# One core, eight batches of two-way attention and a gated convolution block: a new order of the same operations on every engine

## The chip, the cores and the metric

The kernel runs on one core of a Trainium2 chip. The metric is device time in microseconds (us) of one execution; the profile's times count from the start of its span. Five engines work side by side, each through its own list of instructions in order: TensorE (PE in the profile, its weight loads PEld), VectorE (DVE), ScalarE (ACT), GpSimd (POOL) and SyncE (SP), which here only issues transfers.

## The reference

The inputs are x (8 batches, 8 heads, 512 rows, 64 columns) and state (8, 8, 32, 64). Each head reads the state with its rows and the rows with its state, both by a softmax; the 544 rows of each batch then pass a hidden layer, a convolution over three neighbouring rows, a gate and an output layer.

```
scores = scale * x @ state.T ; a = softmax(scores) ; xread = a @ state
scores2 = scale * state @ x.T ; a2 = softmax(scores2) ; sread = a2 @ x
x = concatenate([xread, sread])          (8, 544, 512), heads side by side
h = maximum(x @ w_in, 0)                 (8, 544, 1024)
conv_out = sum over k of conv_w[k] * h shifted by k - 1 rows
out = (h * sigmoid(conv_out)) @ w_out    (8, 544, 512)
```

## The kernel before

All work is written first as a plan of 1,673 operations (class Plan), each a function with its engine, what it reads and what it writes. Two tables at the head of the file turn the plan into a program. ORDER lists the operations by number in the order in which they are issued; each engine, SP among them, keeps the part of the list that is its own. A number with a v gives an operation to VectorE that otherwise is ScalarE's, and -n stands for idle multiplications on TensorE of n times 128 columns, with no use for the result (function fill, line 231). BANKS says which of the eight PSUM banks each PSUM tile takes, in the order of the tiles. Waits follow from these tables: an instruction waits for what it reads, and for the last reader of the buffer or bank that it overwrites.

The weights come first (w_load, line 255; five small operations on ACT and DVE for each of 17 pieces), with the attention of batches 0 to 3 beside them. For each batch b the second softmax (scores2) goes through these steps:

- scores (PE, line 323), keep_scores (ACT, line 208), top (DVE, line 352), exp2 (ACT, line 361).
- For batches 4 to 7 the exponentials are turned on a round trip through DRAM, two tiles per batch, 2b and 2b+1: turn (DVE transposes 32x32 blocks, line 378, tile tv), away (SP issues the transfer far<-tv, line 382), and lay (SP issues the transfer e2t<-far, line 386, which waits for that away to land).
- x_load (SP, line 315, tile xx, two halves of 512 KB per batch, two buffers), then read (PE, line 399, tile ps_r) multiplies xx with both tiles e2t of its batch. The batches come to read in the order 0, 2, 1, 3, 5, 7, 6, 4.
- divide, read_flip and read_flipped bring the result to the tile sr, and state_hidden (PE, line 660) makes the hidden rows of the state from it.

The first softmax (softmax, lines 475 to 499) goes over 1024 columns on DVE, with one exponential and one copy on ACT. state_product (PE, line 593) multiplies the state with w_in in its place, so that hidden (PE, line 675, six matmuls) needs only the softmax and that product.

The main body are 64 steps i = 8b + f, one per batch and block f of 128 hidden columns: hidden on PE, relu (ACT, line 214), middle (ACT, line 208, or DVE), before and behind (DVE, lines 718 and 723), sigmoid (ACT, line 727), gate (DVE, line 732), gate_high (ACT, line 219), gate_low (DVE, line 222), then four times project (PE, line 750, three matmuls), one for each chunk c of 128 rows. After the last block of a batch, end (ACT, line 770, or DVE, line 772) brings the sum of chunk c out of PSUM into a tile o, and store (SP, line 791) sends it to the output. There are two buffers o, so an end waits until the store of an earlier one has landed. The last batch stores halves; its last product (project_part, line 755) writes one half of a bank, and end of the other half reads the same bank.

All transfers but three (conv_w and two of the last stores) are issued by SP, strictly in its own order: a store whose tile is not ready holds up every away, lay and x_load behind it, and an away or lay holds up the stores behind it.

```
    def away(i):
        far[i] = dram.tile([P, S], F32, tag="far", name=f"far_{i}")
        nc.sync.dma_start(far[i], tv[i])

    def lay(i):
        e2t[i] = buf([P, 4, NCH * NS], F32, "e2t", f"e2t_{i}")
        nc.sync.dma_start(e2t[i], far[i].rearrange("(h s) (j m) -> (s j) h m", s=NS, j=4))
```

Of the kernel before, what the change touches and what calls it, by code (L numbers as in the profile page):

```python
# [1011 lines left out]
```

## Time and profile before

| | us |
|---|---|
| three runs: median (lowest to highest) | 365.69 (364.69 to 366.98) |
| the profiled execution, whole | 366.53 |
| its span, first to last instruction | 364.8 |
| busy in the span: PE, PEld, DVE, ACT, POOL | 346.9, 270.7, 318.0, 253.3, 39.4 |

Of the 366.53 us of the profiled execution 1.7 lie around the span. The windows view gives busy time by engine in stretches of the span, the granted clock of TensorE and the share of the transfer engines; the chain follows the work that ended last back to its releasers; the timeline lists instructions in order, with the idle time before them in brackets.

### The profile page before, as it was taken

The page shows a single profiled execution, that of the slowest core. Times are in us where ns is not written, and L with a number is a line of the kernel's source. Part 1 is how long each engine was busy: PE and PEld are TensorE (multiplying, and loading weights), DVE is VectorE, ACT ScalarE, POOL GpSimd, SP SyncE. Part 2 cuts the span into 40 slices and gives each one's busy share as a digit, 9 for nine tenths or more (in the row PEclk, how much of TensorE's full clock was granted, in tenths as well). Part 3 has the DMA queues.
Part 4 walks back from the last instruction along what each step waited for, and adds up shares of the span by engine and source line. Part 5 has one row for each costly group of instructions (what it writes and reads, how often), then busy time and mean ns, then how long its engine had stood idle before and what let it go on. Part 6 is the DMA issues. An engine that isn't in the chain of part 4 may idle for free.

```text
span 364.8 us, 6597 instructions
## 1 busy us (share of the span) xinstructions
PE 346.9 (95%) x2493; PEld 270.7 (74%) x2493; DVE 318.0 (87%) x547; ACT 253.3 (69%) x552; POOL 39.4 (11%) x90
## 2 busy tenths in 40 slices
PE   7899979999899989997699999999999999999995
PEld 4767648788588858874598887887788868888874
DVE  1999997999999987999299999999988987998861
ACT  2999979998767776866475659346885575457632
POOL 1000000140000000412000332001031021021100
PEclk9999999999999999999699999999999999999999
DMA  7999795343320065225210001012000030001105
GB/s 259 397 368 363 249 375 188 108 153 86 123 84 0 35 197 201 70 78 173 89 58 0 2 0 59 1 58 88 30 1 2 0 117 0 0 8 47 63 0 173
DMA packets 19343, 39.24 MB, mean 108 GB/s; under 512 B 1904, under 2 KB 8176, under 8 KB 19312
## 3 DMA queue, kind: packets, MB, share of 16 engines
q1 hardware_dynamic: 18880, 38.54, 30.5%
q8 instruction: 19, 0.31, 0.4%
q10 hardware_dynamic: 432, 0.29, 0.3%
q14 instruction: 12, 0.10, 0.1%
HBM read 27.81 MB, written 11.01 MB: 106 GB/s over the span
## 4 chain that ended last, share of the span: by engine, by line
PE 77%; DMA 9%; DVE 6%; ACT 6%; issue 1%; SPq 1%; DVEq 0%; ACTq 0%
PE acc L750 37%; PE ps_h L675 19%; PE ps_hs L660 4%; PE ps_h L682 4%; PE acc_t L750 3%; DMA out<-o 3%; DMA xx<-xn 2%; PE ps_u L593 2%; PE ps_r L399 2%; DMA far<-tv 2%; PE ps_s L323 2%; DMA raw<-w_in 2%; PE acc_c L750 1%; DVE t L723 1%; DVE t L718 1%; ACT hc L259 1%
## 5 line engine op out<-in xcount | busy, mean ns | idle before, releaser
L750 PE MATMUL acc<-wo,g 128*128 128x512 f32 x723 | 173.2, 390 | 0.0
L750 PEld LDWEIGHTS acc<-wo,g 128*128 128x128 f32 x723 | 135.0, 188 | 28.5 <-DVE g L222 0.4
L675 PE MATMUL ps_h<-a,u 128*128 128x512 f32 x336 | 84.5, 398 | 0.0
L675 PEld LDWEIGHTS ps_h<-a,u 128*128 128x128 f32 x336 | 64.1, 193 | 15.9 <-ACT hs L664 0.8
L727 ACT ACTIVATE t<-t 128x512 f32<-128x512 f32 x64 | 39.8, 629 | 23.5 <-DVE t L723 23.1
L219 ACT ACTIVATE g<-t 128x512 fp32r<-128x512 f32 (+1 forms) x62 | 37.8, 618 | 18.5 <-DVE t L732 12.7
L718 DVE SCALAR_TENSOR_TENSOR t<-h,cw,t 128x511 f32<-128x511 f32 x64 | 47.1, 744 | 1.3 <-ACT t L208 1.2
L723 DVE SCALAR_TENSOR_TENSOR t<-h,cw,t 128x512 f32<-128x512 f32 (+1 forms) x64 | 47.0, 745 | 0.7
L222 DVE TENSOR_TENSOR g<-t,g 128x512 fp32r<-128x512 f32 (+1 forms) x62 | 41.3, 669 | 5.8 <-ACT g L219 5.7
L732 DVE SCALAR_TENSOR_TENSOR t<-t,h 128x512 f32<-128x512 f32 (+1 forms) x64 | 41.8, 662 | 4.7 <-ACT t L727 4.6
L214 ACT ACTIVATE h<-ps_h 128x512 f32<-128x512 f32 x58 | 34.2, 595 | 13.0 <-PE ps_h L675 11.5
L208 ACT ACTIVATE t<-h,cw 128x512 f32<-128x512 f32 x52 | 37.3, 722 | 2.9 <-DVE h L216 1.9
L693 POOL COPY hs<-h 128x1 f32<-128x1 f32 x40 | 17.0, 440 | 173.1 <-ACT h L214 149.8
L770 ACT ACTIVATE o<-acc 128x512 f32<-128x512 f32 (+1 forms) x30 | 16.3, 558 | 17.0 <-DMA out<-o 9.6
L693 POOL COPY h<-hs 128x1 f32<-128x1 f32 x40 | 17.6, 461 | 58.7 <-DVE t L732 37.2
L222 DVE TENSOR_TENSOR u<-ps_u,u 128x512 fp32r<-128x512 f32 x28 | 18.8, 679 | 3.2 <-ACT u L219 3.2
L399 PEld LDWEIGHTS ps_r<-xx,e2t 128*32 128x32 f32 x512 | 8.3, 115 | 17.6 <-DMA e2t<-far 3.8
L399 PE MATMUL ps_r<-xx,e2t 128*32 128x64 f32 x512 | 9.9, 229 | 11.0 <-DMA e2t<-far 5.2
L219 ACT ACTIVATE u<-ps_u 128x512 fp32r<-128x512 f32 x28 | 16.0, 595 | 1.1 <-PE ps_u L593 0.8
L660 PEld LDWEIGHTS ps_hs<-sr,wi 128*128 128x128 f32 x128 | 14.9, 192 | 1.4 <-ACT at L208 0.8
L660 PE MATMUL ps_hs<-sr,wi 128*128 128x128 f32 x128 | 15.3, 276 | 0.0
L259 ACT ACTIVATE hc<-raw 128x512 f32<-128x512 f32 (+1 forms) x17 | 11.2, 664 | 5.5 <-DMA raw<-conv_w 2.8
(103 smaller groups left out, 402.7 us busy)
## 6 DMA issues: line engine op xcount, KB each, us to landing
xt<-xT SPq DMA_DIRECT2D x16, 512.0 KB, 6.9
xx<-xn SPq DMA_DIRECT2D x16, 512.0 KB, 5.8
out<-o SPq DMA_DIRECT2D x27, 256.0 KB, 2.1
raw<-w_in SPq DMA_DIRECT2D x8, 512.0 KB, 7.3
raw<-w_out SPq DMA_DIRECT2D x8, 512.0 KB, 7.5
far<-tv SPq DMA_DIRECT2D x8, 256.0 KB, 2.8
e2t<-far SPq DMA_DIRECT2D x8, 256.0 KB, 3.1
out<-o SPq DMA_DIRECT2D x6, 128.0 KB, 1.8
```

The costliest lines, as they stand in the source:

```text
L208: A.activation(dst, src, AF.Copy, scale=scale)
L214: A.activation(dst, src, AF.Relu, scale=0.5)
L219: A.activation(hi, src, AF.Copy)
L222: engine.tensor_tensor(lo, src, hi.bitcast(F32), op=ALU.subtract)
L660: PE.matmul(ps_hs[m, f][:, :NT], wi[:, k, f * P:(f + 1) * P], sr[m][:, k, :], start=(k == 0), stop=(k == NK - 1))
L675: PE.matmul(ps_h[i], u[j][:, g, fs], a[k][:, g, :], start=(n == 0), stop=(n == 3 * NG - 1))
L693: G.tensor_copy(dst, src)
L718: V.scalar_tensor_tensor(t[:, 1:], h[:, :S - 1], cw[:, f, 0:1], t[:, 1:], op0=ALU.mult, op1=ALU.add)
L723: V.scalar_tensor_tensor(t[:, :n], h[:, 1:n + 1], cw[:, f, 2:3], t[:, :n], op0=ALU.mult, op1=ALU.add)
L727: A.activation(tt[i], tt[i], AF.Tanh, scale=0.25)
L732: V.scalar_tensor_tensor(tt[i][:, :n], tt[i][:, :n], 1.0, hd[i][:, :n], op0=ALU.add, op1=ALU.mult)
L750: PE.matmul(acc, g[j][:, cs], wo[:, k, f, :], start=(f == 0 and n == 0), stop=(f == end and n == 2))
```

## The change

Both tables are replaced; nothing else in the file differs. The operations are the same but for idle multiplications: 12 entries instead of 6, all of them in the first 20 us of work, six more instructions of 128 columns. VectorE takes 24 operations from ScalarE in both (9 middle, 7 relu, 7 end and 1 keep_scores, where it was 12, 6, 5 and 1). The start of the new order and two lines of the tables:

```diff
 ORDER = """
-99 100 -1 121 -5 -7 102 101 103 122 1 -1 125 15 126 -1 127v 143 0 104 16 18 17 144 19 128 21 22 24 151 145 3 2 152 153
+0 -1 -5 122 121 99 100 -7 -1 -1 -1 -1 101 102 103 104 -1 1 125 127v 15 16 126 128 17 143 18 151 144 145 21 23 129 19 3
...
-1511 1522v 1462 1508 1477 1523 1492 1520v 1521 1507 1518 1519
+1508 1663 1477 1524 1525 1517 1662 1492 1507 1518 1520v 1521 1519
```

What the change moves is shown at three places. In the names, far_15 and e2t_15 are the round trip of tile 15 (batch 7, tile 1), xx_7_0 is the first half of x for batch 7, and o_1_2_0 is the output tile of batch 1, chunk 2; the last number of a name only counts tiles.

SP in the middle of the program, before, around the two round trips of batch 7:

```order
L382 DMA far_15_1616<-tv_15_1611 128x512
L386 DMA e2t_15_1634<-far_15_1616 128x4x128
L791 DMA out<-o_0_2_0_1231 128x512
L315 DMA xx_7_0_1674<-xn 128x1x1024
L382 DMA far_14_1695<-tv_14_1668 128x512
L791 DMA out<-o_1_2_0_1697 128x512
L386 DMA e2t_14_1741<-far_14_1695 128x4x128
L315 DMA xx_6_0_1794<-xn 128x1x1024
```

The same place in the change:

```order
L382 DMA far_14_1572<-tv_14_1561 128x512
L382 DMA far_15_1600<-tv_15_1587 128x512
L386 DMA e2t_15_1664<-far_15_1600 128x4x128
L386 DMA e2t_14_1681<-far_14_1572 128x4x128
L315 DMA xx_7_0_1689<-xn 128x1x1024
L791 DMA out<-o_1_1_0_1715 128x512
L791 DMA out<-o_1_2_0_1776 128x512
```

Both far transfers of batch 7 now come first, then both e2t, then xx, and the stores of batch 1 stand behind them; before, a store of batch 0 and one of batch 1 stood between.

SP at the two round trips of batch 4 (tiles 8 and 9), before:

```order
L382 DMA far_8_2039<-tv_8_2037 128x512
L386 DMA e2t_8_2044<-far_8_2039 128x4x128
L315 DMA xx_4_1_2085<-xn 128x1x1024
L315 DMA xx_4_0_2091<-xn 128x1x1024
L382 DMA far_9_2095<-tv_9_2088 128x512
L386 DMA e2t_9_2097<-far_9_2095 128x4x128
L791 DMA out<-o_2_3_0_2116 128x512
L791 DMA out<-o_2_2_0_2172 128x512
```

The same place in the change:

```order
L382 DMA far_9_1975<-tv_9_1973 128x512
L791 DMA out<-o_1_3_0_1826 128x512
L382 DMA far_8_2042<-tv_8_1908 128x512
L315 DMA xx_4_0_2060<-xn 128x1x1024
L791 DMA out<-o_2_0_0_2071 128x512
L386 DMA e2t_8_2121<-far_8_2042 128x4x128
L315 DMA xx_4_1_2157<-xn 128x1x1024
L386 DMA e2t_9_2178<-far_9_1975 128x4x128
L791 DMA out<-o_2_2_0_2175 128x512
```

Both far transfers have moved ahead of the xx halves; one store of batch 2 (o_2_0) now stands ahead of both e2t transfers.

DVE from the first transpose of batch 4 on, before:

```order
L378 STREAM_TRANSPOSE tv_8_2037<-e2_8_2020 128x512
L723 SCALAR_TENSOR_TENSOR t_24_1959<-h_24_1954,cw_79,t_24_1959 128x512
L222 TENSOR_TENSOR u1_3_1_1970<-ps_u_3_1_1_1972,u0_3_1_1969 128x512
L475 STREAM_TRANSPOSE af_4_2071<-at_4_980 128x1024
L723 SCALAR_TENSOR_TENSOR t_25_1943<-h_25_1934,cw_79,t_25_1943 128x512
L364 TENSOR_SCALAR s2_6_1609<-s2_6_1609 128x2
L365 RECIPROCAL s2_6_1609<-s2_6_1609 128x2
L807 SCALAR_TENSOR_TENSOR ss_0_0_1051<-ss_0_0_1051,hs_84 128x128
L718 SCALAR_TENSOR_TENSOR t_26_1998<-h_26_1916,cw_79,t_26_1998 128x511
L222 TENSOR_TENSOR gts1_0_0_2080<-ss_0_0_1051,gts0_0_0_2079 128x128
L378 STREAM_TRANSPOSE tv_9_2088<-e2_9_2056 128x512
L732 SCALAR_TENSOR_TENSOR t_24_1959<-t_24_1959,h_24_1954 128x512
```

DVE in the change, from the second transpose of batch 4 on:

```order
L378 STREAM_TRANSPOSE tv_9_1973<-e2_9_1903 128x512
L475 STREAM_TRANSPOSE af_4_2014<-at_4_989 128x1024
L732 SCALAR_TENSOR_TENSOR t_23_1765<-t_23_1765,h_23_1565 128x512
L800 SCALAR_TENSOR_TENSOR ss_0_0_1240<-hs_84,cw_79,ss_0_0_1240 128x128
L222 TENSOR_TENSOR g1_22_1956<-t_22_1796,g0_22_1955 128x512
L222 TENSOR_TENSOR g1_23_2023<-t_23_1765,g0_23_2022 128x512
L718 SCALAR_TENSOR_TENSOR t_27_2031<-h_27_1905,cw_79,t_27_2031 128x511
L222 TENSOR_TENSOR u1_3_1_1959<-ps_u_3_1_1_1961,u0_3_1_1958 128x512
L718 SCALAR_TENSOR_TENSOR t_24_2057<-h_24_1945,cw_79,t_24_2057 128x511
L222 TENSOR_TENSOR u1_3_1_1959<-ps_u_3_1_0_1960,u0_3_1_1958 128x512
L807 SCALAR_TENSOR_TENSOR ss_0_0_1240<-ss_0_0_1240,hs_84 128x128
L723 SCALAR_TENSOR_TENSOR t_24_2057<-h_24_1945,cw_79,t_24_2057 128x512
```

Before, the second transpose (tv_9) comes ten instructions behind the first and one gate follows before PE needs the result; in the change work of three batches follows it. In ORDER the last DVE operation on which PE depends ahead of its read of batch 4 is now the 18th behind that transpose, and was the first. The same count is 11 instead of 5 for batch 7, 12 instead of 7 for batch 6 and 33 instead of 14 for batch 5.

Three more places in words. On PE nine operations (6.4 us of PE work at the durations of the profile) now lie between the last read of batch 1, which frees the buffer of x for batch 3, and the read of batch 3; there were seven (5.2 us). At the beginning the idle entries ahead of the first scores are eight instead of four, and PE sums the exponentials of the first half of batch 0 before it shifts the scores of the second. At the end the last two evacuations of chunk 2 of batch 7 come one after the other behind the last product, ACT's first and then DVE's; before, DVE's came ahead of that product, and the product waited for it.

## Rows read from the trace of the kernel before

**Rows 1.** The page, busy time of TensorE, its share and instructions.
```profile
PE 346.9 (95%) x2493; PEld 270.7 (74%) x2493; DVE 318.0 (87%) x547; ACT 253.3 (69%) x552; POOL 39.4 (11%) x90
```

**Rows 2.** The windows view; the first line names the columns.
```profile
core 0: us, PE busy (x) PEld busy (x) DVE busy (x) ACT busy (x) POOL busy (x), PEclk, DMA share, GB/s
0.00:8.00 8.00, 6.57 (x46) 3.82 (x47) 1.12 (x5) 1.62 (x3) 1.33 (x8) 1.00 0.73 242
8.00:48.00 40.00, 38.46 (x579) 27.43 (x578) 39.13 (x76) 39.62 (x92) 0.00 (x0) 1.00 0.95 345
48.00:58.00 10.00, 7.66 (x110) 5.00 (x109) 7.50 (x15) 7.67 (x20) 0.00 (x0) 1.00 0.92 347
...
94.00:100.00 6.00, 4.52 (x116) 2.33 (x101) 5.53 (x10) 3.93 (x12) 0.00 (x0) 1.00 0.25 75
...
130.00:146.00 16.00, 14.28 (x135) 10.98 (x134) 12.50 (x20) 11.29 (x28) 0.00 (x0) 1.00 0.57 190
...
166.00:184.00 18.00, 12.78 (x133) 9.14 (x132) 10.31 (x19) 9.56 (x22) 2.13 (x4) 0.81 0.44 132
184.00:250.00 66.00, 66.00 (x333) 54.92 (x332) 64.41 (x100) 41.93 (x82) 9.32 (x20) 1.00 0.08 31
```

**Rows 3.** The chain that ended last: start us, us, what.
```profile
45.94 7.61 DMA xx<-xn
...
131.36 2.96 DMA out<-o
...
138.25 4.57 DMA out<-o
...
166.52 6.80 DMA far<-tv
173.34 3.12 DMA e2t<-far
...
178.43 2.56 PE ps_h L675 x6
181.20 2.03 PE ps_h L675 x6
...
194.07 1.36 PE ps_h L675 x6
```

**Rows 4.** The timeline of PE: start, us, instruction, count, idle before it.
```profile
7.70 0.49 PE L231 MATMUL idle<-zeros 128*128 128x128 f32 x2
...
98.09 1.10 PE L399 MATMUL ps_r<-xx,e2t 128*32 128x64 f32 x64 [1.48 <-ACT af L485]
...
136.96 1.10 PE L399 MATMUL ps_r<-xx,e2t 128*32 128x64 f32 x64 [1.72 <-DMA e2t<-far]
...
168.92 1.95 PE L593 MATMUL ps_u<-wi,st 64*32 64x512 f32 x32
172.78 0.43 PE L399 MATMUL ps_r<-xx,e2t 128*32 128x64 f32 x16 [1.92 <-issue]
176.51 1.51 PE L399 MATMUL ps_r<-xx,e2t 128*32 128x64 f32 x48 [3.30 <-DMA e2t<-far]
...
361.06 0.62 PE L755 MATMUL acc<-wo,g 128*128 128x256 f32 x3 [0.85 <-DVE o L772]
```

**Rows 5.** The timeline of DVE at the end.
```profile
360.25 0.76 DVE L772 TENSOR_SCALAR o<-acc 128x256 f32<-128x256 f32 x2 [3.63 <-DMA out<-o]
```

**Rows 6.** The transfers by line: count, size, median us from issue to landing.
```profile
xx<-xn SPq DMA_DIRECT2D x16, 512.0 KB, 5.8
out<-o SPq DMA_DIRECT2D x27, 256.0 KB, 2.1
far<-tv SPq DMA_DIRECT2D x8, 256.0 KB, 2.8
e2t<-far SPq DMA_DIRECT2D x8, 256.0 KB, 3.1
```

**Rows 7.** The waits view: total us, times, longest.
```profile
ACT o L770 <- DMA out<-o: 9.6, 3, 6.4
```

More of the change, by code (lines that the diff above doesn't have):

```diff
@@ L62 @@
 BANKS = """
-01234567102341742035760314560321450627450672547157311305310357103571530755145620713146520725020714
-2312546353643615423601361057316702523542246502104276514076521427017652425547604102542642173273246
+01234567120342341075074163754217306420746350730132072071372370132730127132341560237431602560260520
+6375421124010425024561660712507404213417214710604336713065417415716503474704170634356401172021732
 """
 ORDER = """
-99 100 -1 121 -5 -7 102 101 103 122 1 -1 125 15 126 -1 127v 143 0 104 16 18 17 144 19 128 21 22 24 151 145 3 2 152 153
@@ L110 @@
-1170 1157 1193 426 1141 1142 424 1098 1224 1143 1238 1145 1166 1572 1158 1171 1182 1144 1239 1159 418 419 1321 1241
-1183 1146 420 421 1184 1574 1575 1276 1242v 1161 1172 1194 1197 1185 458 1173 1176 1198 1227 1228 1196 1195 1199 1209
-1210 1200 1240 1174 1186 1187 1225 1181 1291 1576 1577 1212 1160 1578 1292 1201 1306 1188 1175 1226 1277 1147 1213
-1229 1214 1162 1278 1177 1192 1215 1216 1230 1202 1203 1294 1231 1211 1579 1280 1281 1217 1261 1232 1218 1580 1207
-1582 1191 1583 1282 1243 1244 1189 1206 1221 1262v 1307 1283 1233 1245 1246 1265 1204 1284 1219 1190 1205 1220 1235
@@ L115 @@
-1266 1247 1248 1234 459 1263 1222 1285 1310 1250 1286 1237 1573 1581 1249 1236 1267 1268 1584 1585 1251 1269 1322v
-1324 1323 1270 1257 1271 1308 1252 1311 1255 1312 1325 1326 460 1279 463 464 1309 465 461 1256 1313 1253 1586 1336
-1337 1338 1258 1293 1259 1351 1366 1327 1314 1272 1340v 462 1328 1341 1389 1352 1353 1342 1274 1587 1588 1404 1295
-1595 1296 1297 1298 1260 1287 1339 1329 468 1390 1299 1596 466 1419 469 1392 1264 1405 1275 1290 1343 1289 1597 1598
-1354 1273 1300 1301 1305 1420v 1423v 1304 1589 1599 1600 1601 1344 1315 1603 1604 1407 1605 1606 1316 1319 1320 1288
@@ L120 @@
-1303 467 1434 1367 1391 1607 1330 1602 1393 1355v 1356 1357 1424 1358 1254 1318 1302 1331 1334 1394 1422 1608 1421
-1609 1370v 1371 1406 1611 1612 1359 1345 1346 1317 1368 1425 1613 1426 1449 1614 1372 1335 1350 1590 1373 1427 1435v
-1408v 1615 1616 1409 1360 1333 1348 1594 1450 1410 1361 1464 1617 1411 1412 1349 1438 1332 1610 1436 1465v 1395 1467
-1635 1439 1440 1374 1375 1636 1637 1347 1362 1638 1639 1396 1640 1428 1397 1618 1376 1413 1479 1641 1468v 1480 1429
-1451 1619 1620 1437 1365 1363 1364 1398 1399 1378 1494 1383 1402 1377 1621 1384 1414 1452 1453 1466 1592 1380 1469
@@ L125 @@
-1591 1401 1622 1623 1624 1625 1400 1416 1481 1483v 1627 1626 1441 1415 1628 1379 1431 1442 1387 1388 1454 1593 1470
-1629 1630 1403 1443 1455 1456 1417 1631 1632 1432 1444 1446 1457 1633 1385 1386 1484 1634 1485 1482 1495 1471 1643
-1458 1418 1433 1644 1645 1486 1430 1445 1459 1646 1472 1473 1647 1474 1496 1461 1487 1448 1460 1463 1369 1447 1476
-1478 1498v 1648 1649 1642 1650 1497 1651 1475 1499 1488 1489 1490 1500 1501 1502 1652 1653 1654 1655 1656 1657 1658
-1491 1503 1504 1506 1659 1505 1662 1663 1516 1514v 1381 1515 1660 1661 1382 1512 1513 1517 1493 1509 1524 1525 1510
@@ L130 @@
-1511 1522v 1462 1508 1477 1523 1492 1520v 1521 1507 1518 1519
+0 -1 -5 122 121 99 100 -7 -1 -1 -1 -1 101 102 103 104 -1 1 125 127v 15 16 126 128 17 143 18 151 144 145 21 23 129 19 3
+22 24 152 146 25 -1 -1 -1 4 147 5 148 9 130 -1 6 26 11 131 153 20 149 135 7 10 12 133 8 13 154 155 156 27 470 476 33
+201 35 28 30 29 34 477 471 2 14 478 200 134 36 472 31 136 157 190 193 39 51 191 132 473 204 205 150 37 32 498 206 38
+474 158 539 207 40 524 42 194 525 41 45 43 52 54 475 208 160 159 47 46 526 44 53 499 500 48 511 209 528v 502 49 529
[36 rows of a table added]
@@ new lines @@
+1122 1568 1569 1123 1129 1130 1133 1570 1134 1137v 1138 1148 416 1126 379 417 1149 1003 1004 1135 1139 382 383 422
+1151 1127 1163 1571 1572 1140 1141 1150 380 381 1152 1153 1136 1164 1142 1178 1179 1180 1154 1143 1165 1208 1223 1167
+1168 425 426 1238 1574 1182v 1155 1181 1156 423 1157 1098 1209v 1210 1193 424 1239 1575 1169 1170 1240 1158 1183 1351
+420 1144 421 1194 1184 1241 418 1146 1161 1196 1171 1185 1147 1162 1172 1159 419 1186 1291 1145 1173 1195 1166 1224
+1226 1197 1212v 1213 1176 1227 1576 1577 1352 1198 1187 1199 1200 1188 1160 1261 1191 1201 1174 1578 1228 1225 1579
@@ new lines @@
+1175 1202 1214 1215 1177 1262v 458 1229 1203 1242v 1192 1230 1231 1243 1244 1265 1189 459 1216 1232 1580 1321 1322
+1276 1128 1573 1217 1207 1582 1264 1266 1245 1246 1263 1267 1268 1190 1205 1353 1277 1280 1278 1211 1247 1583 1584
+1585 1306 1292 1218 1204 1325 1233 1206 1269 1248 1219 1234 1249 1253v 1279 1295 1293 1296 1307 1254 1355 1356 460 461
+465 1357 1326 1323 463 1327 1220 1235 1281 1221 1236 1586 1324 1328 1329 462 1250 1251 1222 1237 1257 1255 1282 1270
+1271 1258 1256 1336 464 1283 1284 1309 1310 1294 1285 1366 1297 466 1286 1419 1587 1588 1420v 1298 1299 1581 1422 1300
@@ new lines @@
+1308 1252 1259 1311 1312 1595 1596 1389 1367 1390v 1392 1275 1290 1313 1274 1314 1315 1301 1597 1369 1272 1391 1273
+467 1337 1316 1289 1340 1598 1341 1338 1342 1434 1305 1368 1287 1320 1302 1393 1394 1358 1288 468 1404 1343 1359 1317
+1370v 1371 1395 1330 1331 1423v 1335 1344 1304 1319 1599 1600 1601 1396 1397 1405 1354 1303 1318 1333 1345 1398 1424
+1589 1346 1348 469 1449 1360 1361 1494 1421 1372 1373 1406 1590 1425 1408v 1603 1435 1437 1409 1426 1436 1410 1411
+1334 1349 1332 1407 1464 1604 1399 1605 1364 1438 1347 1412 1593 1439 1606 1607 1413 1414 1608 1609 1602 1610 1339
@@ new lines @@
+1350 1365 1465v 1468 1440 1611 1612 1613 1466 1450 1374 1614 1615 1362 1451 1453 1616 1495v 1375 1479 1376 1377 1441
+1363 1467 1260 1469 1380 1617 1635 1427 1378 1454 1402 1428 1636 1637 1638 1387 1455 1388 1639 1640 1401 1416 1417
+1379 1403 1641 1442 1498 1499 1480v 1618 1619 1620 1594 1429 1496 1500 1432 1418 1400 1470 1621 1622 1483v 1484 1471
+1381 1415 1382 1433 1472 1443 1431 1444 1456 1591 1481 1457 1458 1448 1447 1623 1624 1485 1625 1626 1446 1430 1445
+1459 1460 1461 1592 1473 1627 1628 1501 1385 1452 1629 1630 1631 1632 1633 1502 1383v 1486 1643 1644 1482 1645 1646
@@ L131 @@
+1384 1474 1487 1386 1497 1634 1642 1503 1476 1647 1475 1488 1489 1490 1648 1649 1504 1462 1651 1652 1463 1478 1653
+1654 1505 1510v 1512v 1511 1655 1656 1493 1509 1657 1522v 1513 1523 1650 1658 1659 1491 1506 1660 1661 1514 1515 1516v
+1508 1663 1477 1524 1525 1517 1662 1492 1507 1518 1520v 1521 1519
 """
```

5 lines of the change are left out of this document (removed), and 72 rows, old and new, of the table ORDER.

## The prediction

> **What bounds the kernel now.** I read the page first: TensorE is busy for 346.9 of 364.8 us, VectorE for 318.0, ScalarE for 253.3 [rows 1]. That TensorE is nearly full says little by itself, since its matmuls are pipelined; so the windows view came next, to see where each engine stops. From 8 to 48 us PE, DVE and ACT are all over 38 of 40 us busy, and from 184 to 250 PE has no gap and DVE lacks 1.6 of 66 us [rows 2]. The reader is to see that these stretches leave nothing for an order to gain. The loss is in four short stretches, and the chain names what ends each: a transfer, every time [rows 3].
>
> - 48 to 58 us: xx (7.61 us) for batch 3. PE is idle for 2.34 of the 10 us, DVE for 2.50 [rows 2].
> - 94 to 100 us: batch 5, whose lay(10) stands behind a store and an away on SP. PE is idle for 1.48, DVE for 0.47.
> - 130 to 146 us: batch 7. SP holds a store of batch 0 behind away(15) and e2t, and lay(14) behind a store of batch 1. ACT's end waits for output buffers, 9.6 us in three waits, 6.4 in the longest [rows 7]; PE is idle for 1.72 (at the read of batch 7, on e2t [rows 4]), DVE for 3.50.
> - 166 to 184 us: batch 4. Away(9) landed after 6.80 us, with two xx issued just ahead of it, then e2t took 3.12 [rows 3]. The two pieces of the read waited 1.92 and 3.30 us [rows 4]; PE lacks 5.22 us, DVE 7.69.
>
> In the last the granted clock averages 0.81, against 1.00 in the others named [rows 2]: PE ran at its upper level, 2.4 GHz, before it stood idle at the read, and the chain's two hiddens after it took 2.56 and 2.03 us where one normally takes 1.36 [rows 3]. That is 1.20 + 0.67 = 1.87 us more than the idle time.
>
> PE's loss is then 2.34 + 1.48 + 1.72 + 5.22 = 10.76, with the slow hiddens 12.6 us. DVE's is 2.50 + 0.47 + 3.50 + 7.69 = 14.2. Both engines stay in lockstep up to about 250 us, so what is to be had lies between these, 13.5.
>
> **The change part by part.** Nothing is removed, and the operations that change between ACT and DVE are 24 either way; busy time stays within a microsecond. Everything turns on whether each round trip gets longer cover.
>
> Batches 5, 7 and 6. A DVE instruction takes 318.0 / 547 = 0.58 us on average [rows 1]. Behind the last turn of the batch DVE now does 33, 11 and 12 instructions ahead of the last one that PE's read needs, instead of 14, 5 and 7: 19, 6.4 and 7.0 us, instead of 8.1, 2.9 and 4.1. An undisturbed round trip is 2.8 + 3.1 = 5.9 us [rows 6]. So all three are covered, where batches 5 and 7 lay near or under it or had a store between. With both fars and both e2ts of batch 7 in one row on SP, no store stands between them any more. Batch 6 did not show a wait before and should not now. I count the 1.48 and the 1.72 of PE as gone, and the waits of ACT with them, because the stores of batch 0 now go ahead of away(14).
>
> Batch 4. The count goes from 1 to 18, 10.4 us. But the limit here is SP, not DVE: xx_4_1 and lay(9) are issued only behind the store of chunk 0 of batch 2. From the last project of that chunk to the read PE has six projects, three hiddens, two state products and a read_flip. A hidden is 1.36 [rows 3], a project, half as many matmuls of the same shape, 0.68, two state products 1.95 [rows 4]: 4.1 + 4.1 + 1.95 = 10.1 us. Against it stand the evacuation (0.4 to 0.8, since half a tile takes 0.38 [rows 5]; I take 0.6), SP's issues (which no row shows; 0 to the 1.92 that a piece of the read waited for issue [rows 4]; I take 1.5, near the only row) and a transfer between 3.1 [rows 6] and 6.80 [rows 3], the longest that one took here behind two xx: 5.2 to 8.9 us with the values taken, 9.5 at the worst. I take it as covered, with 0.6 us to spare at the worst. Then the clock has no reason to fall, and the 1.87 goes too. If the cover fails, each microsecond late comes back as one of PE, and the slow hiddens with it.
>
> That 6.80 is a transfer of 256 KB, of which the median is 2.8 [rows 6]; behind two xx it waits its turn. The Trainium skill ("DMA: Bandwidth & Descriptors", section "Queues, rings and completion order") says that descriptors of one queue start in order on an engine, while different queues take turns packet by packet. All of these transfers are SP's, and the row agrees. This speaks against the change, which issues xx_4_1 directly ahead of lay(9): by the rule lay(9) takes the 6.80 and not the 3.1, the spare shrinks from 4.9 us to 1.2, and the sum stays.
>
> Batch 3. Its xx can start when the last read of batch 1 frees the buffer; PE work up to the read of batch 3 grows from 5.2 to 6.4 us. An xx takes 5.8 in the median and took 7.61 here, in the stretch where the transfer engines are 0.92 busy [rows 2, 3, 6]. So about 1.2 of the 2.34 goes for certain, the rest only if the transfer is quicker. I count it as gone in the 13.5 and put what may stay into the new waits below.
>
> Beginning and end. Four more idle entries stand ahead of the first scores; a pair takes 0.49 [rows 4], so they cost 1.0, less what PE would have waited there anyway. I take 0.5, between 0 and 6 x 0.25 = 1.5 for all six. At the end the wait of 0.85 for DVE's evacuation goes [rows 4], and one of 0.38 (half of 0.76 [rows 5]) comes in series behind the last product: -0.4, between -0.85 and +0.4. Together +0.1.
>
> New waits. In the new order end of chunk 0 of batch 2 waits for a store behind away(13), and end of chunk 2 for one behind away(9); behind each ACT has the relu and gate_high that PE and DVE wait for. x of batch 7 reaches its read with under 2 us to spare. No row shows these; the bounds are 0, and the sum of what such places cost before, 14. Below nothing they can't be, as what they replace is already counted as gone. I take 3.0: the rest of batch 3 (1.1), and 2 us in the other places. That lies near the low end because the nearest undisturbed row, 184 to 250 us, loses 0 on PE and 1.6 on DVE [rows 2].
>
> Sum: 366.53 (the profiled execution) - 13.5 + 3.0 + 0.1 = 356.1 us. That execution stands 0.84 above the median; from the median the same sum gives 355.3. I predict the middle, 355.7.
>
> **The rivals.**
>
> *Half comes back.* PE, DVE and ACT are full at the same time for long stretches [rows 2], so each order must hand over within less than a microsecond, and the new one brings forward turns that other work has to make room for: gates and behinds that PE waits for come later. For it: DVE's 7.69 us in batch 4 are more than PE's 5.22, so DVE's debt is not all PE's to win. Against it: PE has no gap from 184 to 250 at the same kind of work. New waits of half of 13.5 give 366.53 - 6.75 + 0.1 = 359.9 us; 358.5 to 362.
>
> *The change doesn't do what it says.* The waits move instead of going: e2t of batch 4 late behind xx, x of batch 3 as late as before, one stall of ACT. If new waits of 10 to 15 us replace 13.5, the time is 363 to 368, about 366. For it: SP still has every store, away and lay in one row, and DMA is 0.92 to 0.95 busy up to 58 us. Against it: the cover of three of the four places at least doubles or rises above 5.9 us.
>
> *Slower: stores in SP's row.* Away(13) waits for its turn on DVE, and the store of chunk 0 of batch 1 behind it can't start; ACT then stands at end of chunk 0 of batch 2, as it stood for 6.4 us before [rows 7]. The same at away(9) and end of chunk 2, and since the store of chunk 0 of batch 2 is then late, lay(9) is late too, and the read of batch 4 waits as it did, 5.22 + 1.87 and more, up to 6.80 + 2.0 = 8.8. Sum: 2 x 6.4 + 8.8 = 21.6, and the time 366.53 - 13.5 + 21.6 + 0.1 = 374.7 us. It decides from the point at which the new waits exceed 13.5. Against it: all three must happen, and the turns are issued early.
>
> **How the numbers follow.** The forecast (351 to 358.5) gets 0.62, half back 0.17, the waits moved 0.13, the slower one 0.08. About 1% is what a measurement of this kernel can tell from no change; that is below 362.0 and above 369.3. Faster is then 0.62 + 0.16 (most of half back) = 0.78, within it 0.01 + 0.13 = 0.14, slower 0.08. The low end of the range, 351, is 366.53 - 14.2, less what batch 3's and the end's bounds still give (0.85), rounded down for a median below this execution; the high end, 363, takes in half back and the beginning of the waits moved. Left out are most of the moved waits and the slower case, with a little below 351: two in ten.
>
> **What would show it right or wrong.** Right: the reads of batches 5, 7 and 4 start within 0.5 us of PE's operation before them and that of batch 3 within 1.2; no wait of ACT's end for an output transfer over 1 us up to 200 us; granted clock 1.00 through the hiddens behind the read of batch 4, each 1.36; the hiddens of the same block some 10 us earlier from there to the end; DVE's idle time up to 190 us under 5. Wrong: a wait over 2 us at the read of batch 4 on e2t, which would mean that SP's row and not DVE's cover was the limit; an ACT wait on output transfers at the ends of batch 2; PE gaps of 0.2 to 0.5 us spread over 200 to 300 us, which would be half back; or a first hidden later by over 1 us, which would be the idle entries.

## The result, and the profile after

The changed kernel takes 353.69 us in the median of four runs (353.47 to 353.78), the kernel before beside it 365.72 us (364.69 to 366.98): a ratio of 0.9669, 95% interval 0.9638 to 0.9699, so 3.0 to 3.6% less. The profiled execution took 353.71 us with a span of 351.2.

The page of the changed kernel, busy time by engine, answers to [rows 1]:

```profile
PE 345.0 (98%) x2505; PEld 269.0 (77%) x2505; DVE 319.0 (91%) x547; ACT 253.8 (72%) x552; POOL 34.3 (10%) x90
```

The span is 13.6 us shorter. TensorE (PE) was idle for 364.8 - 346.9 = 17.9 us of it and is now for 351.2 - 345.0 = 6.2; its busy time fell by 1.9, although it has twelve more records of idle matmuls, two for each of the six. 11.7 + 1.9 is the whole of the 13.6. VectorE and ScalarE are as busy as before. The medians differ by less, 12.0: the profiled execution of before stood 0.8 above its median, and around the span lie 2.5 us in that of the changed kernel, 1.7 in that of before.

The windows view of the changed kernel, columns as in [rows 2], in stretches chosen so that each holds the reads that the stretches of [rows 2] hold (48 to 58: batch 3; 94 to 154: batches 5, 7 and 6; 154 to 171: batch 4):

```profile
8.00:48.00 40.00, 38.69 (x594) 27.93 (x579) 38.85 (x74) 38.69 (x90) 0.00 (x0) 1.00 1.00 366
48.00:58.00 10.00, 10.00 (x121) 6.70 (x120) 9.53 (x18) 10.00 (x27) 0.00 (x0) 1.00 0.93 312
58.00:94.00 36.00, 36.00 (x246) 27.85 (x252) 35.86 (x64) 33.13 (x80) 0.96 (x2) 1.00 0.41 141
94.00:154.00 60.00, 60.00 (x484) 47.25 (x469) 59.03 (x90) 46.84 (x108) 1.95 (x6) 1.00 0.30 101
154.00:171.00 17.00, 16.95 (x159) 12.40 (x158) 16.83 (x28) 13.87 (x31) 1.43 (x7) 1.00 0.44 128
171.00:237.00 66.00, 66.00 (x335) 54.87 (x334) 64.62 (x101) 41.75 (x84) 8.89 (x19) 1.00 0.07 24
```

PE has no idle time from 48 to 154 us and 0.05 us from 154 to 171, where before it lacked 2.34, 1.48, 1.72 and 5.22; the granted clock is 1.00 in all of them, and was 0.81 around batch 4. One long stretch says it at a glance:

```profile
20.00:337.00 317.00, 316.95 (x2207) 248.19 (x2192) 302.35 (x508) 238.39 (x517) 32.97 (x82) 1.00 0.29 99
```

From 20 to 337 us PE stands still for 0.05 us.

The groups by line, PE, the read: busy time and mean ns, then the idle time ahead of it. First the kernel before, then the changed one:

```profile
L399 PE MATMUL ps_r<-xx,e2t 128*32 128x64 f32 x512 | 9.9, 229 | 11.0 <-DMA e2t<-far 5.2 <-DMA xx<-xn 2.3 <-issue 1.9
```

```profile
L399 PE MATMUL ps_r<-xx,e2t 128*32 128x64 f32 x512 | 8.9, 221 | 0.0
```

These two rows are the result in short: 11.0 us of waiting at the reads, 0.0 now. The 11.0 are the 2.34 of batch 3, the 8.42 of [rows 4] and 0.21 at batch 6. At batch 5 the row of [rows 4] names ACT, whose af was done by 97.2 us; e2t landed at 98.00, just ahead of the read at 98.09.

The timeline of PE at batch 4, changed kernel, answers to the rows from 168.92 us on in [rows 4]:

```profile
157.55 4.37 PE L675 MATMUL ps_h<-a,u 128*128 128x512 f32 x18
...
164.57 1.95 PE L593 MATMUL ps_u<-wi,st 64*32 64x512 f32 x32
166.45 1.10 PE L399 MATMUL ps_r<-xx,e2t 128*32 128x64 f32 x64
167.48 1.65 PE L675 MATMUL ps_h<-a,u 128*128 128x512 f32 x6
```

No bracket stands at the read. The three hiddens ahead of it take 4.37 us together, and the one behind it 1.65 with its pipeline's end; the pair behind the read before took 2.56 and 2.03 [rows 3].

The transfers that the reads wait for, changed kernel, as in [rows 6], and the waits of ACT's and VectorE's end:

```profile
xx<-xn SPq DMA_DIRECT2D x16, 512.0 KB, 5.4
...
far<-tv SPq DMA_DIRECT2D x8, 256.0 KB, 2.2
e2t<-far SPq DMA_DIRECT2D x8, 256.0 KB, 3.3
```

```profile
ACT o L770 <- PE acc L750: 7.9, 5, 3.1
...
DVE o L772 <- ACT o L770: 4.2, 2, 2.5
...
DVE o L772 <- PE acc L750: 3.5, 2, 2.3
```

The 9.6 us that ACT's end waited for output transfers [rows 7] are gone from the list; what is left are waits for PE and for ACT.

### The profile page after: what moved, and what is told of

Its sections match the earlier page's. It is cut to its first block, busy times and chain, and to the rows that moved or that the text cites. A ratio compares the mean times of both kernels' runs of the same rounds, so it can differ in the third digit from the quotient of the medians.

```text
span 351.2 us, 6639 instructions
## 1 busy us (share of the span) xinstructions
PE 345.0 (98%) x2505; PEld 269.0 (77%) x2505; DVE 319.0 (91%) x547; ACT 253.8 (72%) x552; POOL 34.3 (10%) x90
## 4 chain that ended last, share of the span: by engine, by line
PE 85%; DVE 5%; DMA 4%; ACT 4%; issue 1%; SPq 0%; DVEq 0%; ACTq 0%
PE acc L750 41%; PE ps_h L675 21%; PE ps_hs L660 4%; PE ps_h L682 4%; PE ps_u L593 4%; DMA raw<-w_in 3%; PE ps_r L399 2%; PE ps_s L323 2%; PE acc_t L750 2%; PE acc_c L750 2%; PE acc L764 2%; DMA raw<-conv_w 1%; DVE g L222 1%; ACT g L219 1%; DVE t L732 1%
## 5 line engine op out<-in xcount | busy, mean ns | idle before, releaser
L675 PE MATMUL ps_h<-a,u 128*128 128x512 f32 x336 | 82.2, 391 | 0.0
L675 PEld LDWEIGHTS ps_h<-a,u 128*128 128x128 f32 x336 | 62.7, 188 | 14.0 <-ACT gts L219 0.8
L208 ACT ACTIVATE t<-h,cw 128x512 f32<-128x512 f32 x55 | 38.9, 722 | 1.8 <-DVE h L216 1.3
L693 POOL COPY hs<-h 128x1 f32<-128x1 f32 x40 | 18.4, 475 | 173.1 <-ACT h L214 145.6
L770 ACT ACTIVATE o<-acc 128x512 f32<-128x512 f32 (+1 forms) x28 | 15.5, 569 | 9.4 <-PE acc L750 7.9
L693 POOL COPY h<-hs 128x1 f32<-128x1 f32 x40 | 15.3, 396 | 45.2 <-DVE t L732 31.5
L593 PE MATMUL ps_u<-wi,st 64*32 64x512 f32 x224 | 14.1, 596 | 0.7 <-ACT u L208 0.7
L682 PE MATMUL ps_h<-p,u 128*128 128x256 f32 x64 | 14.7, 382 | 0.0
```

The lines of the kernel that those rows point to most:

```text
L208: A.activation(dst, src, AF.Copy, scale=scale)
L675: PE.matmul(ps_h[i], u[j][:, g, fs], a[k][:, g, :], start=(n == 0), stop=(n == 3 * NG - 1))
L693: G.tensor_copy(dst, src)
```

## The experiments

An operation stands by its name and arguments, in the order in which its engine issues it; ORDER has it by number. The ratios are to the kernel before, run beside them; its median lay between 365.0 and 365.5 us in the three series of four kernels. Kernels made from the changed one are set against its 353.69. The tables of most of these kernels take one or two lines less, so the same line of code has a slightly lower number in their rows.

**One transpose earlier, before.** VectorE's second transpose of batch 4 is moved forward.

```diff
 turn(8)  behind(24)
+turn(9)
 state_low(3,1,1) att_flip(4) behind(25) norm2(6) side_gate(0,0) before(26) side_low(0,0)
-turn(9)
 gate(24)
```

> The kernel before, with one instruction of VectorE moved: the second transpose of batch 4 (tv_9) stands one instruction behind the first instead of ten, so it should end near 162.4 us instead of 166.0. SP's order is as before, where the away of that tile stands behind lay(8), which waits until 164.8 for far_8, and behind both xx of batch 4. Theory SP (SP's row set the wait of batch 4): away(9) is still issued near 166.3 us, takes about 6.8 us, and PE's two waits at the read stay 5.2 us with the slow hiddens behind them; time unchanged, 365.7 within 1. Theory cover (what counts is how many VectorE instructions lie between the transpose and the read, as the prediction counted them): 3.6 us of the wait go, and the time falls to 361 to 363.

Measured: 365.43 us, ratio 0.9991 (0.9956 to 1.0026): between 1.6 us gained and 0.9 lost, so not the 3.6 of the theory of cover. The transfer of that tile in this kernel, and PE's waits at the reads:

```profile
L380 SPq DMA_DIRECT2D far<-tv x1: 590/590/590, 166.9 to 166.9; - x1
...
DMA to landing us min/median/max: 6.0/6.0/6.0
```

```profile
PE ps_r L397 <- DMA e2t<-far: 4.9, 3, 3.1
```

The transposes are done by 163.6 us, yet the away goes out at 166.9 behind two xx and takes 6.0 us; e2t lands at 175.8, against 176.5 before, and the read still waits 3.1 us for it. (The wait of its first piece is 0.36 us, not 1.92, mostly because PE comes to the read 1.1 us later in this execution.) The theory that cover on VectorE is what counts falls for this place of the kernel before.

**SP's order alone at batch 4, before.**

```diff
 away(8)
+x_load(4,1) x_load(4,0)
 lay(8)
-x_load(4,1) x_load(4,0)
 away(9) lay(9)
```

> The kernel before, with SP's order alone changed at batch 4: both xx go out right behind away(8), ahead of lay(8), instead of between lay(8) and away(9); the second transpose stays late. Theory SP: the xx land by 168, away(9) goes out near 166.2 without two fresh xx ahead of it and lands by 169, e2t by 172.2; PE comes to the read near 170.6, so the wait is 1.5 to 2 us instead of 5.2, and the clock may stay up: gain 3.5 to 5.5, time 360 to 362. Theory cover: without an earlier transpose the round trip is as late as it was, gain under 1.5 us, time 364 to 366.

Measured: 362.12 us, ratio 0.9922 (0.9884 to 0.996), 1.5 to 4.2 us gained of 365.0. The same transfer and the read:

```profile
L380 SPq DMA_DIRECT2D far<-tv x1: 337/337/337, 167.3 to 167.3; - x1
...
DMA to landing us min/median/max: 3.5/3.5/3.5
```

```profile
173.96 0.88 PE L397 MATMUL ps_r<-xx,e2t 128*32 128x64 f32 x48 [1.68 <-DMA e2t<-far]
...
175.27 1.65 PE L673 MATMUL ps_h<-a,u 128*128 128x512 f32 x6 [0.17 <-ACT o L768]
...
176.78 1.62 PE L673 MATMUL ps_h<-a,u 128*128 128x512 f32 x6
```

The transpose is as late as before, but the away takes 3.5 us, since it goes out 3.2 and 4.6 us behind the two xx, not 0.6. PE waits 1.68 us, and the hiddens behind the read are at full clock. Less than was expected (3.5 to 5.5), with its sign and its place as expected.

**Both at batch 4, before.** turn(9) as in the first, and on SP:

```diff
 away(8)
-lay(8)
 x_load(4,1)
+away(9)
 x_load(4,0)
-away(9)
+lay(8)
 lay(9)
```

> The kernel before, with both changes at batch 4: the early transpose, and SP's order away(8), xx, away(9), xx, lay(8), lay(9). Theory of the prediction: PE's wait of 5.2 us and the 1.9 us of slow hiddens go completely, 7.1 us, time 358.6, range 357.5 to 360. Theory half (VectorE's lag of 7.7 us there isn't all PE's to win, PE then waits for VectorE or ScalarE in the following 30 us): 3 to 4 us, time 361.5 to 363. If both single changes gain nothing and this one gains all, both conditions are needed.

Measured: 359.96 us, ratio 0.9842 (0.9778 to 0.9906), 3.4 to 8.1 us gained; at the upper end of the expected 357.5 to 360. PE's wait at that read is 0.24 us in its timeline. Against SP's order alone these are some 2 us more in the medians (the intervals overlap), from the early transpose together with the away that SP can then send earlier; the transpose by itself showed no gain.

**The clock alone.** Six matmuls whose result the read overwrites, in read (line 392):

```diff
             ps_r[b] = bank(f"ps_r_{b}")
+            for _ in range(6 if b == 4 else 0):
+                PE.matmul(ps_r[b], zeros, zeros.unsqueeze(1).broadcast_to([P, 4, P]), start=True, stop=True)
         for g in range(NG):
```

> The kernel before, with six idle multiplications of 512 columns on PE ahead of the first matmul of the read of batch 4, into the bank that the read then overwrites: they fill about 5.1 of the 5.2 us in which PE stands still there, and the transfers and their waits stay as they are. Theory clock (the two slow hiddens come from the idle time ahead of them): granted clock 1.00 through 176 to 183 us, hiddens of 1.36 us, 1.9 us less: 363.8, range 363 to 364.5. Rival: the hiddens are slow for another reason, or VectorE's and ScalarE's late results set the pace behind the read, and the time stays at 365.7.

Measured: 364.75 us, ratio 0.9973 (0.9935 to 1.0011). The interval holds both -1.9 and 0, so the time doesn't settle it. The profile does for the place. Its timeline of PE:

```profile
173.66 5.42 PE L397 MATMUL ps_r<-zeros 128*128 128x512 f32 x12
179.01 1.10 PE L401 MATMUL ps_r<-xx,e2t 128*32 128x64 f32 x64
180.04 0.33 PE L414 MATMUL ps_f<-ident,rr 128*128 128x128 f32 x1
180.13 1.64 PE L677 MATMUL ps_h<-a,u 128*128 128x512 f32 x6
181.60 0.27 PE L414 MATMUL ps_f<-ident,rr 128*128 128x128 f32 x1
181.63 1.63 PE L677 MATMUL ps_h<-a,u 128*128 128x512 f32 x6
```

PE is busy all through the wait (5.42 us), the windows view has the granted clock at 1.00 from 166 to 184 us, and the two hiddens take 1.50 and 1.46 us to the start of what follows. From the landing of e2t (178.47 us) to the first state_hidden behind them are 4.6 us, against 6.6 before (176.47 to 183.07), and from there to the end of the span 181.7 in both. Of the kernel before a matmul of these hiddens took up to 775 ns, twice the 389 that is usual, here at most 476: the lower level of the clock, 1.2 GHz. So the slow hiddens came from the standstill ahead of them, and the 2.0 us are kept to the end in this execution. It lost as much earlier, at batch 3:

```profile
48.00:58.00 10.00, 7.45 (x97) 4.28 (x96) 7.30 (x14) 5.98 (x15) 0.00 (x0) 0.83 0.89 345
```

The granted clock is 0.83 there, and was 1.00 before [rows 2]; read and scores behind the wait for xx take 1.93 and 1.76 us instead of 1.10 and 1.09, and PE comes to the state_hidden behind them 1.8 us later (58.55 against 56.71). So its span is 364.8 us, as before.

**SP's order alone at batch 7, before.**

```diff
 lay(10)
+store(0,2,0)
 x_load(7,1) last_store away(15) lay(15)
-store(0,2,0)
 x_load(7,0) away(14)
+lay(14)
 store(1,2,0)
-lay(14)
```

> The kernel before, with SP's order alone changed around batch 7: the store of chunk 2 of batch 0 goes out right behind lay(10) instead of behind lay(15), and lay(14) right behind away(14) instead of behind the store of chunk 2 of batch 1. Theory PE (only PE's wait for e2t counts): the wait of 1.3 to 1.7 us at the read of batch 7 goes, 1.0 to 1.7 us gained, 363.5 to 364.2. Rival ACT (the 9.6 us in which ACT's end waited for output buffers held up VectorE and PE as well): 2.5 to 3.5 us gained, 361.7 to 362.7, since VectorE was idle for 3.5 us there. Rival nothing: what is late next (VectorE's gate_low, ACT's gate_high) takes the wait's place and the time stays within 0.5 us of before.

Measured: 365.1 us, ratio 0.9999 (0.9972 to 1.0027): nothing. Its read row and ACT's waits:

```profile
L397 PE MATMUL ps_r<-xx,e2t 128*32 128x64 f32 x512 | 10.4, 240 | 10.6 <-DMA e2t<-far 3.4 <-ACT o L768 3.2 <-DMA xx<-xn 1.6
```

```profile
ACT o L768 <- DMA out<-o: 10.6, 3, 5.6
```

The read of batch 7 now waits 3.22 us, and what ends the wait is no longer e2t but ACT's end: its bank comes free only when ACT has brought out chunk 1 of batch 1, and that end waits 4.1 us (0.7 before) for the output buffer of the store that lay(14) was put ahead of. The store went out at 132.3 us instead of 131.4 and took 4.65 us instead of 2.96. But e2t is hardly earlier either: lay(14) went out 1.9 us earlier, at 131.8, took 4.57 us instead of 3.11 and landed at 136.4, against 136.8 before. PE came to the read at 134.45, so without ACT's wait it would have stood for 1.9 us all the same. What made both transfers slower here is not shown. ACT's wait is the slower rival's mechanism, at another chunk than the one that the prediction named.

**One transpose earlier at batch 7, before.**

```diff
 before(17)
+turn(14)
 att_top(3) behind(17) att_sub(3)
-turn(14)
 gate(17)
```

> The kernel before, with one instruction of VectorE moved at batch 7: the second transpose (tv_14) goes right behind the exponential that it reads, ahead of the top of the first softmax of batch 3, a behind and its subtraction, so that it ends near 126.6 us instead of 128.6. SP's order is as before. Theory cover: away(14) goes out near 127.5, behind xx_7_0, lands by 131, lay(14) goes out behind the store of chunk 2 of batch 1 at 131.5 and lands near 134.7, before PE comes to the read at 135: PE's wait of 1.7 us goes and 1.5 to 2 us are gained, 363.5. Theory SP: lay(14) still stands behind that store, whose tile ACT makes at the same time as before, and what the transpose brings is lost there or in VectorE's softmax, which starts 0.9 us later: within 0.7 us of before.

Measured: 365.65 us, ratio 1.002 (0.9992 to 1.0048): nothing, and the cover theory falls here too. The xx that SP issues just ahead, the away of that tile, and the transposes:

```profile
L313 SPq DMA_DIRECT2D xx<-xn x1: 541/541/541, 127.4 to 127.4; - x1
...
DMA to landing us min/median/max: 5.8/5.8/5.8
```

```profile
L380 SPq DMA_DIRECT2D far<-tv x1: 628/628/628, 128.0 to 128.0; - x1
...
DMA to landing us min/median/max: 5.9/5.9/5.9
```

```profile
L376 DVE STREAM_TRANSPOSE tv<-e x2: 709/710/712, 123.5 to 126.4; 128x512 f32<-128x512 f32 x2
```

The transposes end at 127.1 instead of 128.6 us, but xx_7_0 went out at 127.4 and takes 5.8 us, and the away behind it takes 5.9: landed at 134.0, against 133.7 before.

**PE's order alone at batch 3, before.** The three letters of BANKS that belong to these operations change places with them.

```diff
+scores(5)
 read(3,0) read(3,1)
-scores(5)
 read_flip(1)
```

> The kernel before, with PE's order alone changed at batch 3: the scores of batch 5 (16 matmuls, 1.1 us) go ahead of the read of batch 3 instead of behind it, so that PE has that work in the 1.4 to 2.5 us in which it waits for xx. Theory PE: the wait shrinks by 1.1 us and the time with it: 0.7 to 1.2 us less, 364.3 to 364.8. Rival: the read's result is then late for ACT and the state, or the scores wait for x themselves, and nothing is gained.

Measured: 365.18 us, ratio 0.999 (0.9962 to 1.0019), so between 1.4 us gained and 0.7 lost; the expected gain is inside, and so is nothing. PE's wait for xx went completely; waits of 1.43 and 3.38 us at batch 4 and 1.16 at batch 7 were left (1.92, 3.30 and 1.72 before). In the two profiled executions the span is 1.6 us shorter, but that of before stands 0.8 above its median. What became of the freed time stays open.

**Three places, and four, before.** The first has batch 4 as above, batch 7's SP order, and at batch 5 away(10) ahead of store(0,0,0) and both lays ahead of store(0,1,0). The second adds batch 7's earlier transpose and batch 3's scores. SP at batches 5 (both) and 7 (the second):

```diff
 away(11)
+away(10)
 store(0,0,0) x_load(5,1)
-store(0,1,0)
 lay(11)
-away(10)
 lay(10)
+store(0,1,0)
+store(0,2,0)
 x_load(7,1) last_store
 away(15)
+away(14)
 lay(15)
-store(0,2,0)
+lay(14)
 x_load(7,0)
-away(14)
 store(1,2,0)
-lay(14)
```

> The kernel before, with the orders at batches 4 and 7 of the two earlier kernels, and at batch 5 away(10) and lay(10) ahead of the stores of chunks 0 and 1 of batch 0. Nothing is changed on PE, on ACT or at the beginning; on VectorE one transpose. Theory additive (what is freed at one place is kept to the end, as PE is then the bound): batch 4 5.0 to 7.1, batch 7 1.0 to 1.7, batch 5 1.4, together 7.4 to 10.2: 355 to 358. Rival lockstep (VectorE or ScalarE becomes the bound once two or three waits are gone): less than 6 us, over 359.

> The kernel before with all four places mended in the fewest moves: batch 4 and 5 as in the kernel with three places (357.3 us), batch 7 with the early transpose and both far and both e2t transfers in one row ahead of xx_7_0 and the stores, batch 3 with the scores ahead of the read. Theory: PE's remaining waits at batch 7 (1.6) and 3 (1.1 of 1.5) go, 2.0 to 2.7 us less: 354.6 to 355.3, and the spread of the runs falls below 1 us as PE no longer waits for transfers. The changed kernel's 353.7 is then explained to within 1 to 1.5 us (the end, 0.4 to 0.9, and what is left of batch 3, 0.4). Rival: the rest of the gain of the change comes from its other order of the gates and projects, and this kernel stays at 356.5 or more.

Measured: 357.3 us, ratio 0.9806 (0.9748 to 0.9865), for three; 357.18, ratio 0.9777 (0.9749 to 0.9804), for four. The first as expected; the second 2 us over, and in the range of its rival (356.5 or more). So 8.0 us are had by moving a few transfers, one batch of scores and two transposes; the 3.5 us from there to the changed kernel come from the rest of the new order, and no run takes that apart. The read rows of both:

```profile
L397 PE MATMUL ps_r<-xx,e2t 128*32 128x64 f32 x512 | 9.2, 221 | 4.0 <-ACT o L768 1.6 <-ACT corner L689 1.5 <-DMA e2t<-far 0.9
```

```profile
L397 PE MATMUL ps_r<-xx,e2t 128*32 128x64 f32 x512 | 9.2, 221 | 2.9 <-ACT o L768 0.9 <-DMA xx<-xn 0.8 <-DMA e2t<-far 0.6
```

2.9 us are left at the reads, among them a new wait of 0.9 for ACT's end, and at the end the 0.8 us for VectorE's evacuation that the changed kernel doesn't have. PE is idle for 355.4 - 344.6 = 10.8 us of the span of the kernel with four places, 4.6 more than in the changed one, and its span is 4.2 us longer; that says where the 3.5 us stand, not which move brings them. The runs spread by 0.4 us (356.85 to 357.25) instead of several, as expected.

**The slower rival made to happen.** The changed kernel, SP:

```diff
 store(2,0,0)
+store(2,2,0)
 lay(8) x_load(4,1) lay(9)
-store(2,2,0)
```

> The changed kernel, with SP's order alone changed at batch 4: the store of chunk 2 of batch 2 goes ahead of lay(8), xx_4_1 and lay(9), which then wait for its tile until about 165.9 us; they went out at 157.4, 158.3 and 158.95 us. This is the mechanism of the slower rival, made to happen at one place. Theory SP: xx lands near 172, e2t near 172.5, PE comes to the read at 166.4 and waits 5.5 to 6.5 us, and the granted clock falls behind it, some 2 us more: 353.7 + 7.5 to 8.5 = 361 to 362. Rival slack (VectorE and ScalarE use the time, and what they are ahead by comes back later): 356 to 359.

Measured: 360.83 us against 353.69 for the changed kernel, 7.1 more. Its timeline of PE:

```profile
170.17 0.66 PE L398 MATMUL ps_r<-xx,e2t 128*32 128x64 f32 x16 [3.33 <-issue]
172.73 1.51 PE L398 MATMUL ps_r<-xx,e2t 128*32 128x64 f32 x48 [1.90 <-DMA e2t<-far]
174.17 2.79 PE L674 MATMUL ps_h<-a,u 128*128 128x512 f32 x6
```

Waits of 3.33 and 1.90 us, the hidden behind them 2.79 instead of 1.65, and the read's two pieces 2.17 instead of 1.10: 7.4 us, where the span grew by 7.9.

**The change with the transpose late.** VectorE, then SP:

```diff
 side_tap(0,0,2)
-turn(9)
 att_flip(4)
...
 att_top(4)
+turn(9)
...
 lay(13)
-away(9)
 store(1,3,0) away(8) x_load(4,0) store(2,0,0) lay(8) x_load(4,1)
+away(9)
 lay(9)
```

> The changed kernel, with the second transpose of batch 4 moved late on VectorE, behind 16 of the instructions that follow it, so that it ends near 162.1 us instead of 151.2; away(9) goes behind xx_4_1 and directly ahead of lay(9) on SP, as it stood before, and nothing holds up what is ahead of it. PE comes to the read at 166.4. Theory cover: away(9) at 162.3 lands at 164.5 to 165.5, e2t at 167.7 to 168.8, PE waits 1.3 to 2.4 us, clock mostly up: 355 to 356.5. If away(9) queues behind xx_4_1 as it did behind two before (6.8 us): e2t at 172, wait 5.6, clock falls, 361. Rival: earlier turns were not needed, time within 0.7 us of 353.7.

Measured: 353.55 us (353.38 to 353.83): no loss against 353.69. The away and the lay of that tile:

```profile
L381 SPq DMA_DIRECT2D far<-tv x1: 328/328/328, 162.2 to 162.2; - x1
...
DMA to landing us min/median/max: 2.0/2.0/2.0
```

```profile
L385 SPq DMA_DIRECT2D e2t<-far x1: 370/370/370, 164.3 to 164.3; - x1
...
DMA to landing us min/median/max: 2.9/2.9/2.9
```

Issued 4.3 us behind xx_4_1 and 0.4 before it landed (157.87 + 4.79 = 162.66 us), away takes 2.0 us and lay 2.9; 0.2 us of wait at the read. Of the 18 instructions of cover on VectorE 16 weren't needed.

**Six idle entries less.** The changed kernel, PE at the beginning; the entries are left out of ORDER.

```diff
 -1 -5 -7 -1
--1 -1 -1 -1
 first_scores(0) first_scores(1) first_flip(0) first_flip(1) first_shift(0)
--1 -1
 -1
```

> The changed kernel without its six additional idle entries on PE: four of 128 columns ahead of the first scores and two behind the first shift are left out. Theory of the prediction: they cost 0.5 us (0 to 1.5), so the time is 352.2 to 353.7, likeliest 353.2. Rival clock: without them PE stands still longer at the beginning, the granted clock falls under 1.00 in the first 25 us, and the time is 0.5 to 2 us longer. Rival nothing: PE waits there for x and for the exponentials anyway, the same time within 0.2.

Measured: 352.91 us (352.43 to 353.8), 0.8 less than the changed kernel in another series; ratio to the kernel before 0.9664 (0.9634 to 0.9695), which overlaps 0.9638 to 0.9699. The first hidden starts 0.67 us earlier in its profile, and the granted clock is 1.00 from 8 to 30 us. It is the fastest kernel here, clearly against the one before; against the changed one the two intervals don't separate it.

## Why the prediction was right, and where its steps were not

355.7 us was predicted, 353.69 measured, inside 351 to 363; faster, and by 12.0 us where 10 was forecast.

**The place of the loss.** Right. The waits at the four reads and the slow hiddens were counted at 10.76 + 1.87 = 12.6 us of PE. The waits are gone to the last tenth (the two read rows), and the hiddens are at full clock.

**Between PE's 12.6 and VectorE's 14.2.** The step took 13.5 because VectorE had lost more than PE. Its number was met, but by luck: all of the gain stands in PE's rows, of which 12.6 was too small a count. The waits at the reads were 11.0, with the 0.21 of batch 6; the hiddens' group of the page fell by 2.3 us (84.5 to 82.2), and the read's by 1.0 (9.9 to 8.9), most of it at batch 4, where its two pieces took 1.94 instead of 1.10. That is 14.3, against 14.0 in the span (13.6, and 0.4 more lost at the beginning and the end).

**New waits, 3.0 us.** This is the term that was mis-sized: 0.0 at all reads. Of it 1.1, for what would stay at batch 3, came from an xx of 7.61 us [rows 3]; in the changed kernel the later half took 5.5 and landed at 52.8, and PE came to that read at 53.9 us. The other 2 were for the ends of batch 2, which found their buffers free, and for xx_7_0, which landed 2.3 us ahead of its read.

**The cover counted on VectorE.** This step failed: it named a wrong cause. It priced batches 5, 7 and 6 by how many instructions lie behind the last transpose (0.58 us each) against 5.9 us of round trip. Moving the transpose alone showed no gain at batch 4 and at batch 7 of the kernel before, and moving it back by 16 instructions cost nothing in the changed one. What counts there is what goes out just ahead of the away on SP. Landing times of the same 256 KB: 2.0 us with nothing ahead (tiles 14, 15 and 9 in the changed kernel) or 4.3 us behind an xx (tile 9 with the transpose late), 3.5 where lay(8) and the rest of two xx were ahead, 5.9 directly behind one xx, 6.0 and 6.80 [rows 3] directly behind two. In each of the last three it landed 0.6 to 0.7 us after the xx ahead of it. The 5.9 us of the prediction for an undisturbed round trip are medians that hold disturbed ones: 2.0 + 2.9 = 4.9 is what one costs. The changed kernel sends all fars of batches 7 and 4 ahead of the xx (before, one of each pair stood there), and that, more than the count, is what the order brought at batch 4. At batch 7 that isn't shown by itself: the one run that sends both fars there ahead of xx, the kernel with four places, has the earlier transpose too. At batch 5 the kernels with three and four places lose the wait of 1.48 us with VectorE's order as it was, by SP's order alone (PE is busy for all of 94 to 100 us in the first). For batch 6 no run separates the two.

The Trainium skill ("DMA: Bandwidth & Descriptors", section "Queues, rings and completion order") has descriptors of SP's ring consumed in order on each engine; the landings 0.6 to 0.7 us behind the xx ahead agree with it, and here it explained more than the prediction gave it.

**Batch 4 limited by SP.** Right, and closely: a cover of 10.1 us against 5.2 to 8.9, with 4.9 to 1.2 to spare, was forecast. lay(9) went out directly behind xx_4_1:

```profile
L386 SPq DMA_DIRECT2D e2t<-far x1: 544/544/544, 158.9 to 158.9; - x1
...
DMA to landing us min/median/max: 5.3/5.3/5.3
```

It landed at 164.3 us, 0.7 behind xx_4_1; the read started at 166.45, 2.2 later. The transfer lies between the two values of the forecast, 3.1 and 6.80. SP's issues, 1.5 in the forecast, took 2.0 (156.99 to 158.95 us), a little over the bound of 1.92. That it was SP's row was shown from the other side: with the same lays behind one more store the time rose by 7.1 us.

**The clock.** Right, and a little small: 1.87 us forecast from the two hiddens; 2.3 less in their group on the page and 2.0 in the execution in which idle matmuls filled the wait. That the page's busy time fell by 1.9 is near 1.87 by chance, as it holds the slow read (1.0) and 1.5 us more of idle matmuls as well.

**ACT's waits for output buffers.** The 9.6 us were put down to batch 7 (130 to 146 us). Only two of the three waits stand there, 0.7 and 2.5 us (ended at 134.4 and 142.9); the longest, 6.4, ended at 177.1 us: end of chunk 2 of batch 2, whose buffer waited for a store behind lay(9). It was the same wait as PE's at batch 4, seen on another engine, and the prediction's price for the slower rival came from the right row in the wrong place.

**The beginning and the end.** +0.1 was forecast. The first hidden starts 0.75 us later (22.16 against 21.41 in the chains); the wait of 0.85 ahead of the last product is gone; behind PE's last matmul the span goes on for 3.6 us instead of 3.1, since the two evacuations now follow each other. Together +0.4. The six idle entries at 0.5 (0 to 1.5) measured 0.8, within the spread of two series. Their price of 0.25 rests on a misread row: the pair of records in [rows 4] is one entry, not two. The price held all the same: the first 10 idle instructions of the changed kernel (20 records) take 6.30 us and the first 6 of before 5.24, so 0.27 for one more.

**The rivals.** Half coming back: PE is busy for 316.95 of the 317 us from 20 to 337, so nothing did. Waits that only move: not in the change, but one single move, batch 7's SP order, brought a new wait for the old one. The slower one: its mechanism is real and costs 7.1 us at one place; in the changed kernel the store on which all hangs went out at 157.0 us, 9.5 us before PE came to the read.

## What to carry to other kernels

When a transfer that an engine waits for shares a queue with bulk loads, ask first what is issued just ahead of it: the same 256 KB took 2.0 us alone and 6.8 behind two halves of x, and a transpose done 2.7 us earlier on the producing engine brought e2t only 0.6 us forward and showed no gain. Where PE is the bound, as here, its idle time ahead of each group of matmuls and the slow matmuls behind a long standstill add up to the gain almost exactly; one wait mended by itself may bring nothing: at batch 7 of the kernel before neither SP's order nor the earlier transpose did alone.
